# Agent attention with a gated convolution on one core: an earlier place for a four-column copy on GpSimd, another split of the last chunk, and eleven steps moved

## The chip, the cores and the metric

The kernel runs on one core of a Trainium2 chip. That core has five engines, each with its own instruction queue: TensorE (PE in the profile, its weight loads apart as PEld), VectorE (DVE), ScalarE (ACT), GpSimd (POOL) and SyncE (SP), which here issues nearly all DMA transfers. An engine works through its queue in order; semaphores order the engines against each other. The metric is the device time of one execution in microseconds; lower is better.

## The reference

There are 4 batches of 12800 tokens with 128 channels and 49 agent vectors. Agents attend over keys and values, queries attend over agents, and the result goes through a causal gated convolution of five taps and two projections:

```python
a2k = sm(agents, k); agent_v = a2k @ v      # 49 x 128 for a batch
x = sm(q, agents) @ agent_v                 # 12800 x 128 for a batch
gate_pre = sum(conv_w[k] * xp[:, k:k+S] for k in range(5))   # xp: x behind 4 rows of zeros
out = (1 / (1 + exp(-gate_pre)) * (x @ w_val)) @ w_out
```

`sm` is a softmax over scaled scores. All inputs are float32 (the weights of the second part arrive as float64).

## The kernel before

**Units.** A batch is cut into 10 units of 1280 tokens. Steps are named by a letter, the batch and the unit. `k1.4` takes scores of keys (16 matmuls, L376). `v1.4` exponentiates them and accumulates the agents' values (L480). `q1.4` takes scores of queries and makes their softmax: a 32x32 transposition on DVE (`sT`, L386), a maximum (`qmx`, L745), a subtraction on POOL (`qw`, L750), an exponential on ACT (L758), sums and a product on DVE (L763 to L772), and then three float16 pieces of the weights in a tile `pt`: a copy on ACT (L779) and two steps on POOL (L784, L794).

**Pairs.** `t1.4` turns `pt` so that agents lie on partitions and tokens along columns. The first four units use TensorE; all others use a DMA transposition issued by SP (L835), into half of a tile `x1`. One `x1` holds a pair of units, 2560 columns, behind 16 columns of padding; there are four such tiles. The convolution looks back over four tokens, so the last four columns of a pair must also stand ahead of the next pair's first column. A copy on POOL (L819; a memset, L816, at a batch's start) does this; it reads what the DMA transposition of the pair's second unit wrote, and so it waits for its landing. In the code this is `halo(s)`, for pair s. Behind the second unit of a pair, two shift DMAs (L884, `x2<-x1`) make five shifted copies of some rows for the whole pair; they too wait for the DMA transposition.

**Chunks.** The second part runs over 100 chunks of 512 tokens, 25 in a batch; five chunks make a pair. For chunk n, `g n` is six matmuls into the PSUM tile `gate` (five of L922, and L926, which reads `x2`) and a tanh on ACT (`th`, L935). `a n` is two matmuls into `val` (L949, L953), a product on DVE (`h`, L962), its float16 part on ACT (`hh`, L968) and the rest on POOL (`hl`, L973). `o n` is three matmuls (L992, L993 and L994, the last reading `hl`), a scaled copy on ACT (`ob`, L1006) and every other time a DMA to the output. The last chunk is cut into two of 256 columns, numbers 99 and 100. `gate`, `val` and `out` are single PSUM banks: `g n` waits for the tanh of the chunk before it, `a n` for its product.

**Folding.** Between two batches, `m` (maxima of the key scores, L425 to L457) and `f` (folding all weights into two stationary operands, L519 to L728) put short chains of DVE, POOL, ACT and PE steps on the way. `m2` first needs the maxima (`kmx`, L411) of all ten key units of batch 2.

**Order.** TensorE's order is written out by hand as one string of steps (`order`, in `tile_agent_attention_gated_conv`). Loads (L369, 640 KB each) follow from it: 11 buffers are filled in the order in which the `k`, `q` and `v` steps stand, and each load waits for the step that last used its buffer. For the other four engines and for SP, a planner (`Plan.order`) walks through the steps with given durations; when several are ready it takes the one with the longest remaining chain. A step becomes ready when all steps named as its reads have been placed, so a name in `reads` changes the order even where the data do not depend on it.

Of the kernel before, what the change touches and what calls it, by code (L numbers as in the profile page):

```python
# [13 lines left out]
ALU = mybir.AluOpType  # L14
# [8 lines left out]
UNIT = 1280  # L23
# [3 lines left out]
CH = 512  # L27
# [12 lines left out]
NT_, NH = 3, 3  # L40
NPT = 4
NX = 4
CUT = 2
NOB = 4
LEAD = 5
MAX_AT = (7, 8)
# [130 lines left out]
def tile_agent_attention_gated_conv(  # L177
# [9 lines left out]
    nc = tc.nc  # L187
    B, C, N = qT.shape
    A = 49
    NU = N // UNIT  # L190
    NCH = N // CH
    NT = B * NCH
# [606 lines left out]
    def on_pe(b, u):  # L799
        g = b * NU + u  # L800
        return g < PE_FIRST or (g < (B - 1) * NU and g % TURN in PE_TURNS)
# [11 lines left out]
    def halo(s):  # L813
        to = x1s[s % NX][:, PAD - HALO : PAD]
        if s * 2 % NU == 0:
            fn = lambda: nc.gpsimd.memset(to, 0.0)  # L816
            read = []
        else:
            fn = lambda: nc.gpsimd.tensor_copy(  # L819
                out=to, in_=x1s[(s - 1) % NX][:, PAD + SEG - HALO : PAD + SEG]  # L820
            )
            read = [(x, (s - 1) % NX, 1) for x in ("x1", "x1b")]

        read.append(("x2", (s - 1) % 3, UNIT, 0))
        add("pool", 0.1, fn, read, [("x1h", s % NX)])

    def transposes(b, u):
        g = b * NU + u
        pt = pts[g % NPT]
        p_ = ("pt", g % NPT)  # L830
        if not on_pe(b, u):
            dst = unit_rows(g)
            add(
                "dma", 1.4,
                lambda: nc.sync.dma_start_transpose(  # L835
                    out=dst.rearrange("p (n i) -> p n i", i=P),
                    in_=pt.rearrange("p n r -> p (n r)"),
                ),
                [(*p_, n) for n in range(3)], [("x1", g // 2 % NX, g % 2)], 2.4,
            )  # L840
            shifts(b, u)
            return
        ps_, at = bank()
        ps = ps_.rearrange("p a b -> p (a b)").bitcast(F16).rearrange("p (h w) -> p h w", h=2)
        dst = unit_rows(g).rearrange("p (h w) -> p h w", h=2)

        def matmuls():
            for n in range(NBLK):
                nc.tensor.transpose(
                    out=ps[:, n // HB, n % HB * P : (n % HB + 1) * P], in_=pt[:, n, :],  # L850
                    identity=ident16,
                )

        add("pe", 0.65, matmuls, [("pt", g % NPT, n) for n in range(3)], [at], key="t")
        add(
            "act", 0.65, lambda: nc.scalar.copy(out=dst[:, 0], in_=ps[:, 0, 0 : HB * P]),
            [at], [("x1", g // 2 % NX, g % 2)],
        )
        add(
            "dve", 0.46,  # L860
            lambda: nc.vector.tensor_copy(out=dst[:, 1], in_=ps[:, 1, 0 : HB * P]),
            [at], [("x1b", g // 2 % NX, g % 2)],
        )
        shifts(b, u)

    def shifts(b, u):

        g = b * NU + u
        if g >= SINGLE and g % 2 == 0:
            return  # L870
        n = 1 if g < SINGLE else 2
        u0 = u + 1 - n
        s = g // 2
        x2, x1 = x2s[s % 3], x1s[s % NX]
        o = (g + 1 - n) % 2 * UNIT
        src = row_keys(s, range(0, g % 2 + 1))
        c = PAD - HALO + o
        for r0, r1, every, us in X2CUTS:
            first = A + (2 if every == 3 else 3 * THREES)
            rows = x1[first : first + 1 + (r1 - r0 - 1) * every : every, c : c + 1]  # L880
            view = [rows.ap[0], (1, TAPS), (1, n * UNIT)]
            add(
                "dma", 0.6,
                lambda r0=r0, r1=r1, rows=rows, view=view: nc.sync.dma_start(  # L884
                    out=x2[r0 * TAPS : r1 * TAPS, o : o + n * UNIT],
                    in_=bass.AP(rows.tensor, rows.offset, view),
                ),
                src, [("x2", s % 3, o + i * UNIT, r0) for i in range(n)], us * n,
            )
        if g % 2 and (g + 1) // 2 < B * NU // 2:  # L890
            halo((g + 1) // 2)


    chunks = [(t // NCH, t % NCH * CH, CH) for t in range(NT - 1)]
    chunks += [(B - 1, N - CH + i * CH // CUT, CH // CUT) for i in range(CUT)]
    banks = {}

    def gates(t):
# [43 lines left out]
    def values(t):  # L942
# [5 lines left out]
        def matmuls():  # L948
# [19 lines left out]
            "act", 0.16 + 0.42 * scale, lambda: nc.scalar.copy(out=hh, in_=h),  # L968
            [("h", t % NH)], [("hh", t % 3)],
        )  # L970
        add(
            "pool", 0.1 + 1.07 * scale,
            lambda: nc.gpsimd.tensor_tensor(out=hl, in0=h, in1=hh, op=ALU.subtract),  # L973
            [("h", t % NH), ("hh", t % 3)], [("hl", t % 3)],
        )

# [101 lines left out]
    for t in range(len(chunks) + 2):  # L1078
# [8 lines left out]
    kinds = {"m": "max", "f": "fold"}  # L1087
    order = (
# [25 lines left out]
    )  # L1114
    first = [(kinds.get(x[0], x[0]), *map(int, x[1:].split("."))) for x in order.split()]
    for w in first:
# [70 lines left out]
```

## Time and profile before

| | us |
|---|---|
| median of 3 runs | 427.45 |
| lowest, highest | 425.69, 428.92 |
| the profiled execution | 425.66 |
| its span, first to last instruction | 423.6 |
| PE busy | 403.9 (95%) |
| ACT busy | 301.5 (71%) |
| DVE busy | 293.3 (69%) |
| POOL busy | 228.2 (54%) |

The profiled execution is 1.79 us below the median. The page gives busy times, the chain of work that ended last, and the waits by engine, line and releaser. The timeline gives single instructions: start, duration, engine, line, operation, tiles, and in brackets the idle time before it and what ended it. A row of SP (SPq) is the issue of a DMA, not its transfer. In the windows, a row is a stretch of time with the busy time of each engine, the clock granted to TensorE (PEclk, 1.00 is full), the busy share of the DMA engines and the rate they moved.

### The profile page before, as it was taken

The numbers are of one execution on the slowest core, as the hardware profiler recorded it, in microseconds if no ns is written. First come the engines' busy times: TensorE is split into PE (matmuls) and PEld (weight loads), VectorE is DVE, ScalarE is ACT, GpSimd is POOL, SyncE is SP. The second block draws the span as 40 slices with busy tenths as digits, with TensorE's granted clock in tenths as the row PEclk, the third lists the DMA queues.
The fourth block names the chain that finished last, engine by engine and source line by source line (L and its number), as shares of the span: only waits on it lengthen the run. The fifth ranks groups of instructions, "written<-read, shape, count | busy, mean of one in ns | idle before, by whom it ended". The sixth has DMA issues, their size and how long they took to land.

```text
span 423.6 us, 10042 instructions
## 1 busy us (share of the span) xinstructions
PE 403.9 (95%) x3907; PEld 197.0 (47%) x3907; DVE 293.3 (69%) x562; ACT 301.5 (71%) x521; POOL 228.2 (54%) x263
## 2 busy tenths in 40 slices
PE   4979999999999999999999899999999989999995
PEld 1358434346555443446555343335555534344443
DVE  3757899867875978667795575767765678676231
ACT  1564568779966777678876486778876567788776
POOL 1002557654657565554566355574366277877553
PEclk9969999999999999999999899999999999999998
DMA  8999999999999999999999999999999977755733
GB/s 320 420 417 411 370 367 353 301 295 310 412 293 283 346 317 362 304 278 356 351 379 324 271 299 370 314 332 302 296 393 322 239 196 161 199 163 176 205 121 124
DMA packets 75129, 127.62 MB, mean 301 GB/s; under 512 B 50466, under 2 KB 50850, under 8 KB 75084
## 3 DMA queue, kind: packets, MB, share of 16 engines
q1 hardware_dynamic: 74940, 126.87, 96.9%
q8 instruction: 30, 0.49, 0.5%
q10 hardware_dynamic: 144, 0.13, 0.2%
q14 instruction: 15, 0.12, 0.1%
HBM read 79.25 MB, written 26.21 MB: 249 GB/s over the span
## 4 chain that ended last, share of the span: by engine, by line
PE 78%; DMA 9%; DVE 8%; ACT 1%; POOL 1%; issue 1%; SPq 0%; POOLq 0%; DVEq 0%; ACTq 0%
PE gate L922 23%; PE sc L376 17%; PE av L480 10%; PE val L949 5%; PE out L992 5%; PE val L953 5%; PE gate L926 5%; PE out L993 4%; DMA ld<-kT 4%; PE out L994 4%; DMA x<-pt 3%; DMA x<-x 2%; DVE h L962 1%; DVE qw L772 1%; DVE qsm L763 1%
## 5 line engine op out<-in xcount | busy, mean ns | idle before, releaser
L973 POOL TENSOR_TENSOR hl<-h,hh 128x512 f16<-128x512 f32 (+1 forms) x101 | 116.9, 1158 | 96.1 <-ACT hh L968 96.0
L922 PE MATMUL gate<-x,stat 128*128 128x512 f16 (+1 forms) x500 | 125.2, 380 | 0.2 <-ACT th L935 0.2
L962 DVE SCALAR_TENSOR_TENSOR h<-th,val 128x512 f32<-128x512 f32 x100 | 67.8, 678 | 66.8 <-PE out L993 26.2
L376 PE MATMUL sc<-ld,ag_sb 128*32 128x320 f32 x1280 | 101.5, 447 | 7.6 <-DMA ld<-kT 7.0
L935 ACT ACTIVATE th<-gate,unscale 128x512 f32<-128x512 f32 x100 | 68.3, 683 | 33.3 <-PE gate L926 31.7
L1006 ACT ACTIVATE ob<-out,oscale 128x512 f32<-128x512 f32 x98 | 67.3, 687 | 21.3 <-PE out L994 20.1
L922 PEld LDWEIGHTS <-stat 128*128 128x128 f16 x505 | 46.3, 97 | 63.7 <-issue 14.8
L968 ACT CAST hh<-h 128x512 f16<-128x512 f32 (+1 forms) x101 | 61.5, 609 | 17.2 <-DVE h L962 16.4
L750 POOL TENSOR_TENSOR qw<-sT,qmx 128x490 f32<-128x490 f32 x40 | 41.4, 1035 | 47.6 <-DVE qmx L745 47.5
L376 PEld LDWEIGHTS sc<-ld,ag_sb 128*32 128x32 f32 x1280 | 36.7, 111 | 59.4 <-issue 25.7
L480 PE MATMUL av<-ld,eT 128*32 128x129 f32 (+1 forms) x1400 | 50.7, 279 | 1.0 <-DVE eT L386 1.0
L480 PEld LDWEIGHTS av<-ld,eT 128*32 128x32 f32 (+1 forms) x1400 | 47.1, 117 | 7.5 <-issue 2.5
L794 POOL TENSOR_TENSOR pt<-qw,pt 128x490 f16<-128x490 f32 x40 | 44.8, 1120 | 3.1 <-ACT pt L779 2.9
L471 ACT ACTIVATE e<-ks,kbias 128x320 f32<-128x320 f32 x80 | 39.3, 554 | 5.4 <-DVE eT L386 3.3
L386 DVE STREAM_TRANSPOSE sT<-sc 128x640 f32<-128x640 f32 x40 | 33.6, 839 | 13.4 <-PE sc L376 12.7
L402 ACT COPY ks<-sc 128x640 f32<-128x640 f32 x40 | 27.7, 691 | 21.2 <-PE sc L376 19.1
L386 DVE STREAM_TRANSPOSE eT<-e 128x640 f32<-128x640 f32 x40 | 33.5, 842 | 9.8 <-ACT e L471 5.2
L926 PE MATMUL gate<-x,stat 95*128 95x512 f16 x100 | 38.3, 383 | 1.5 <-DMA x<-x 1.5
L949 PE MATMUL val<-x,stat 128*128 128x512 f16 x100 | 38.2, 382 | 0.8 <-DVE h L962 0.6
L953 PE MATMUL val<-x,stat 95*128 95x512 f16 x100 | 38.1, 381 | 0.0
L994 PE MATMUL out<-hl,wo 128*128 128x512 f16 x98 | 37.0, 378 | 1.1 <-POOL hl L973 1.1
L992 PE MATMUL out<-hh,wo 128*128 128x512 f16 x98 | 37.3, 381 | 0.1
(130 smaller groups left out, 389.4 us busy)
## 6 DMA issues: line engine op xcount, KB each, us to landing
ld<-kT SPq DMA_DIRECT2D x40, 640.0 KB
ld<-qT SPq DMA_DIRECT2D x40, 640.0 KB
ld<-vP SPq DMA_DIRECT2D x39, 645.0 KB
outT<-ob SPq DMA_DIRECT2D x48, 512.0 KB
x<-x SPq DMA_DIRECT2D x18, 375.0 KB
x<-x SPq DMA_DIRECT2D x18, 100.0 KB
outT<-ob SPq DMA_DIRECT2D x3, 256.0 KB
x<-x SPq DMA_DIRECT2D x4, 187.5 KB
```

What stands on the lines that cost most here:

```text
L376: nc.tensor.matmul(out=out[g * BLK : (g + 1) * BLK, j, 0:GT], lhsT=ag_sb[:, b, j * BLK : (j + 1) * BLK], rhs=src[:, g * GT : (g + 1) * GT] ...
L386: nc.vector.transpose(out=out.rearrange("p n (j i) -> p j n i", j=2), in_=in_.rearrange("p j (n i) -> p j n i", i=BLK),)
L480: nc.tensor.matmul(out=av[o + j : o + j + cols, 0 : C + 1], lhsT=et[:, n, j : j + cols], rhs=vt[:, n, :], start=(u == 0 and n < 2), stop=( ...
L922: nc.tensor.matmul(out=pg, lhsT=stat[:, k, :], rhs=x1[:, c : c + w], start=(k == 0), stop=False,)
L926: nc.tensor.matmul(out=pg, lhsT=stat[0 : TAPS * X2R, TAPS + 1, :], rhs=x2[0 : TAPS * X2R, o2 : o2 + w], start=False, stop=True,)
L935: lambda: nc.scalar.activation(out=th, in_=pg, func=AF.Tanh, scale=unscale[:, 0:1]),
L949: nc.tensor.matmul(out=pv, lhsT=stat[:, TAPS, :], rhs=x1s[(b * NCH + n0 // CH) // 5 % NX][:, PAD + o2 : PAD + o2 + w], start=True, stop=False,
L953: nc.tensor.matmul(out=pv, lhsT=stat[0 : TAPS * X2R, TAPS + 2, :], rhs=x2[0 : TAPS * X2R, o2 : o2 + w], start=False, stop=True,)
L962: lambda: nc.vector.scalar_tensor_tensor(out=h, in0=th, scalar=1.0, in1=pv, op0=ALU.add, op1=ALU.mult),
L968: "act", 0.16 + 0.42 * scale, lambda: nc.scalar.copy(out=hh, in_=h),
L973: lambda: nc.gpsimd.tensor_tensor(out=hl, in0=h, in1=hh, op=ALU.subtract),
L1006: lambda: nc.scalar.activation(out=ob[:, o : o + w], in_=po, func=AF.Copy, scale=oscale),
```

## The change

**The copy of four columns.** `halo(s)` was added behind the shift DMAs of pair s-1, with a read that named these DMAs. It is now added at the start of `transposes` of the pair's first unit, and the name it reads is the `pt` of that unit as written by L794. So the planner places the copy behind POOL's work on the first unit of pair s. What it copies and what it truly waits for (the landing of the second unit of pair s-1) are the same.

**The end.** The two last chunks have 384 and 128 columns, and their `hl` is made by DVE.

**The order.** Eleven places in the string differ, and DMA issues and planner choices follow.

```diff
-CUT = 2
+CUTS = (384, 128)
@@ halo
-        read.append(("x2", (s - 1) % 3, UNIT, 0))
+        read.append(("pt", 2 * s % NPT, 1))
         add("pool", 0.1, fn, read, [("x1h", s % NX)])
@@ transposes
+        if g % 2 == 0 and g:
+            halo(g // 2)
@@ shifts
-        if g % 2 and (g + 1) // 2 < B * NU // 2:
-            halo((g + 1) // 2)
@@ chunks
-    chunks += [(B - 1, N - CH + i * CH // CUT, CH // CUT) for i in range(CUT)]
+    chunks += [(B - 1, N - sum(CUTS[i:]), w) for i, w in enumerate(CUTS)]
@@ values
+        on, eng, us = (nc.vector, "dve", 0.53) if t >= NT - 1 else (nc.gpsimd, "pool", 1.07)
         add(
-            "pool", 0.1 + 1.07 * scale,
-            lambda: nc.gpsimd.tensor_tensor(out=hl, in0=h, in1=hh, op=ALU.subtract),
+            eng, 0.1 + us * scale,
+            lambda: on.tensor_tensor(out=hl, in0=h, in1=hh, op=ALU.subtract),
@@ order (one of the eleven)
-"o35 t1.9 g38 a38 o36 g39 a39 o37 v2.4 t2.0 q2.1 v2.5 g40 a40 o38 q2.2 g41 a41 o39 "
+"o35 t1.9 g38 a38 o36 g39 a39 q2.1 o37 v2.4 t2.0 v2.5 g40 a40 o38 q2.2 g41 a41 o39 "
```

The other ten: `f0` behind `k1.1` instead of ahead of `q0.1`; `q0.6` ahead of `a3 o1`; `q1.4` ahead of `k2.2`; `o44` ahead of `f2 g46 a46`; `k3.2 k3.3` behind `o48`; `o50 k3.5` ahead of `t2.5`; `q2.8 k3.8` ahead of `g56`; `t3.0` ahead of `o62`; `a72` ahead of `o70`; `o96` ahead of `a98`.

Two places show what this makes of the queues. The first is POOL around the copy for pair 8 (units 1.6 and 1.7). The row `hl2` is that of chunk 29, the row `hl0` that of chunk 30; `x1_0` is the tile of pair 8, `x1_3` that of pair 7, `qw1` and `pt1` belong to unit 1.7, `pt0` to unit 1.6. Before:

```order
L794 TENSOR_TENSOR pt0_97<-qw0_89,pt0_97 128x10x49
L973 TENSOR_TENSOR hl1_118<-h1_112,hh1_115 128x512
L973 TENSOR_TENSOR hl2_119<-h2_113,hh2_116 128x512
L750 TENSOR_TENSOR qw1_90<-sT1_86,qmx1_88 128x490
L973 TENSOR_TENSOR hl0_117<-h0_111,hh0_114 128x512
L819 COPY x1_0_101<-x1_3_104 128x4
```

In the changed kernel:

```order
L794 TENSOR_TENSOR pt0_97<-qw0_89,pt0_97 128x10x49
L975 TENSOR_TENSOR hl1_118<-h1_112,hh1_115 128x512
L975 TENSOR_TENSOR hl2_119<-h2_113,hh2_116 128x512
L819 COPY x1_0_101<-x1_3_104 128x4
L750 TENSOR_TENSOR qw1_90<-sT1_86,qmx1_88 128x490
L975 TENSOR_TENSOR hl0_117<-h0_111,hh0_114 128x512
```

The copy moved ahead of the subtraction for query unit 1.7 and of `hl` of chunk 30.

The second place is SP's queue around the pair 9 (units 1.8 and 1.9, tile `x1_1`, shifted into `x20`); `x1_2` belongs to pair 10. Before:

```order
L835 DMA_TRANSPOSE x1_1_102<-pt2_99 128x10x128
L369 DMA ld10_71<-kT 128x1280
L835 DMA_TRANSPOSE x1_1_102<-pt3_100 128x10x128
L1021 DMA outT<-ob3_123 128x1024
L369 DMA ld0_61<-kT 128x1280
L369 DMA ld1_62<-qT 128x1280
L884 DMA x20_105<-x1_1_102 75x1x2560
L884 DMA x20_105<-x1_1_102 20x1x2560
L835 DMA_TRANSPOSE x1_2_103<-pt0_97 128x10x128
L835 DMA_TRANSPOSE x1_2_103<-pt1_98 128x10x128
```

In the changed kernel:

```order
L837 DMA_TRANSPOSE x1_1_102<-pt2_99 128x10x128
L369 DMA ld10_71<-qT 128x1280
L369 DMA ld0_61<-kT 128x1280
L837 DMA_TRANSPOSE x1_1_102<-pt3_100 128x10x128
L1023 DMA outT<-ob3_123 128x1024
L369 DMA ld1_62<-kT 128x1280
L837 DMA_TRANSPOSE x1_2_103<-pt0_97 128x10x128
L886 DMA x20_105<-x1_1_102 75x1x2560
L886 DMA x20_105<-x1_1_102 20x1x2560
L837 DMA_TRANSPOSE x1_2_103<-pt1_98 128x10x128
```

The load of query unit 2.5 moved ahead of the DMA transposition of unit 1.9, and the DMA transposition of unit 2.0 ahead of the two shift DMAs of pair 9.

20 rows, old and new, of the table order are left out of this document.

## The prediction

> **What bounds the kernel now.** I read the page first.
>
> ```profile
> span 423.6 us, 10042 instructions
> PE 403.9 (95%) x3907; PEld 197.0 (47%) x3907; DVE 293.3 (69%) x562; ACT 301.5 (71%) x521; POOL 228.2 (54%) x263
> DMA  8999999999999999999999999999999977755733
> ```
>
> TensorE is busy for 403.9 of 423.6 us; no other engine is above 71%. The change adds no matmul, so it can only act on PE's waits and on the clock PE is granted. The DMA engines are nearly full until four fifths of the span (32 of 40 slices, about 339 us): until then a transfer lands late, and an engine that waits for one waits long. So I asked next for the waits, by engine and releaser (total us, count, longest):
>
> ```profile
> PE sc L376 <- DMA ld<-kT: 7.0, 4, 6.1
> PE gate L926 <- DMA x<-x: 1.5, 1, 1.5
> PE out L994 <- POOL hl L973: 1.1, 1, 1.1
> PE val L949 <- DVE h L962: 0.6, 1, 0.6
> POOL x L819 <- DMA x<-pt: 16.4, 5, 6.0
> ```
>
> The first is mostly the first load (6.1), which stays. The next three are single stops of PE: A (1.5), B (1.1), C (0.6). The last is the copy that the change moves: it holds POOL for 16.4 us in five places, waiting for a DMA transposition.
>
> What a stop costs beyond its length shows in the windows (start, length, busy PE, PEld, DVE, ACT, POOL, clock, DMA share, GB/s):
>
> ```profile
> 233.57:236.98 3.41, 1.91 (x11) 1.02 (x10) 1.10 (x4) 1.43 (x3) 0.53 (x1) 1.00 1.26 190
> 236.98:240.40 3.42, 3.42 (x9) 1.18 (x9) 2.01 (x7) 1.30 (x2) 1.84 (x3) 0.50 1.05 335
> 339.38:342.80 3.42, 2.67 (x24) 1.29 (x24) 1.24 (x6) 1.63 (x4) 3.42 (x5) 1.00 0.56 149
> ```
>
> Stop A lies in the first row. In the next 3.42 us the clock is 0.50 and only 9 matmuls run: half of 3.42, 1.7 us, is lost. Behind B, in the third row, the clock stays at 1.00. So I charge 1.7 us of clock to a stop of 1.5 us or more, nothing to one of 1.1 or less, and A costs 1.5 + 1.7 = 3.2.
>
> The Trainium skill, "TensorE: Matmul & The Clock Gate", section "HAM oscillation — how this bites in real kernels", puts the limit at PE-idle gaps above about 3.4 us. By that rule A would cost 1.5 and the stop forecast below 2.1: the sum stays −1.3, since both lose 1.7, but the second rival below would be worth −3.4 instead of −5.1 and the third +0.5 instead of +2.2. The trace disagrees: a stop of 1.50 us is followed by a window at 0.50.
>
> **The change part by part.** *The copy for pair 8* (units 1.6 and 1.7). POOL, SP, ACT, DVE and PE around it:
>
> ```profile
> 173.60 1.16 POOL L973 TENSOR_TENSOR hl<-h,hh 128x512 f16<-128x512 f32 x1 [0.98 <-ACT hh L968]
> 176.85 1.02 POOL L750 TENSOR_TENSOR qw<-sT,qmx 128x490 f32<-128x490 f32 x1 [2.09 <-DVE qmx L745]
> 178.38 1.16 POOL L973 TENSOR_TENSOR hl<-h,hh 128x512 f16<-128x512 f32 x1 [0.51 <-ACT hh L968]
> 180.02 0.19 POOL L819 COPY x<-x 128x4 f16<-128x4 f16 x1 [0.47 <-issue]
> 179.97 1.68 SPq L884 DMA_DIRECT2D x<-x  x2
> 178.21 0.61 ACT L758 ACTIVATE qw<-qw 128x490 f32<-128x490 f32 x1
> 179.79 0.69 ACT L935 ACTIVATE th<-gate,unscale 128x512 f32<-128x512 f32 x1 [0.97 <-PE gate L926]
> 180.57 0.69 DVE L962 SCALAR_TENSOR_TENSOR h<-th,val 128x512 f32<-128x512 f32 x1 [0.36 <-PE out L993]
> 184.74 0.17 DVE L425 TENSOR_REDUCE m<-kmx 128x2 f32<-128x20 f32 x1
> 185.40 0.27 PE L432 MATMUL av<-ident,m 128*2 128x128 f32 x1
> ```
>
> Before, POOL does the subtraction of unit 1.7 (176.85) and `hl` of chunk 30 (178.38) ahead of the copy, and at 180.02 the copy no longer waits for its source. The shift DMAs wait for the same landing and are issued at 179.97, so I put it there. In the changed kernel the copy stands right behind `hl` of chunk 29, which ends at 173.60 + 1.16 = 174.76: POOL is held for 5.2 us. The subtraction then starts at 180.2 instead of 176.85 and ends at 181.2. ACT's exponential (178.21 before) starts at about 181.25 and ends at 181.86; the tanh of chunk 31 stands behind it and slips from 179.79 to 181.86, by 2.1 us. The product `h` behind it slips from 180.57 to about 183.0. DVE goes through the rest of its queue 2.1 to 2.6 us late up to the maximum at 184.74 (it also gets the exponential's sums later), and PE's L432, at 185.40 directly behind it, waits. Price 2.1 (up to 2.6, down to 0 if the landing comes 3.3 us earlier), and as it is above 1.5 another 1.7 for the clock: **+3.8**. What would cover it is work that PE has ready ahead of L432, and I see none beyond what runs anyway.
>
> *Stop A and SP's queue at pair 9.* SP and PE at the stop, and the same kinds of transfer later in a nearly idle queue:
>
> ```profile
> 220.73 2.63 SPq L835 DMA_TRANSPOSE x<-pt  x1
> 225.49 0.73 SPq L369 DMA_DIRECT2D ld<-qT  x1
> 228.28 1.65 SPq L884 DMA_DIRECT2D x<-x  x2
> 230.04 5.71 SPq L835 DMA_TRANSPOSE x<-pt  x2
> 235.67 0.39 PE L926 MATMUL gate<-x,stat 95*128 95x512 f16 x1 [1.50 <-DMA x<-x]
> 376.80 1.35 SPq L835 DMA_TRANSPOSE x<-pt  x1
> 381.08 1.65 SPq L884 DMA_DIRECT2D x<-x  x2
> ```
>
> The shift DMAs of pair 9 are issued at 228.28 and land at 235.67. Behind them stand two DMA transpositions (230.04); the change puts the first of these, unit 2.0, ahead of the shifts. Its price is not shown alone there: at least the issue of one in the nearly idle queue, 1.35, at most from its issue to the shifts that wait for it, 381.08 − 376.80 = 4.3. I take 2.2, nearer to the issue, since other engines' transfers overlap most of the 4.3. Against it, the copies stand elsewhere and transpositions of neighbouring units no longer go out in pairs, so the queue may run ahead: 0 to 2 us, I take 0.7. Loads keep their place: that of unit 2.5's queries passes one transposition but stood ahead of the shifts before too. So the shifts land at 235.67 + 2.2 − 0.7 ≈ 237.2, between 235.67 + 1.35 − 2 ≈ 235.0 and 235.67 + 4.3 = 240.0.
>
> PE wanted them at 235.67 − 1.50 = 234.17. By the parts above and below it now comes there 0.2 + 3.8 later, at 238.2, behind the landing: A goes, **−3.2**.
>
> The Trainium skill, "DMA: Bandwidth & Descriptors", section "Latency and other measured facts", gives 261 GB/s for a DMA transposition; a unit is 128 x 1280 float16, 0.33 MB, an estimate by that page of 1.26 us. No run here shows one by itself. It would leave the sum as it is, and shorten the wait of the first rival from 2.3 to 1.4.
>
> *Stops B and C.*
>
> ```profile
> 338.78 0.19 POOL L819 COPY x<-x 128x4 f16<-128x4 f16 x1 [5.99 <-DMA x<-pt]
> 338.93 2.27 POOL L973 TENSOR_TENSOR hl<-h,hh 128x512 f16<-128x512 f32 x2
> 341.15 0.61 POOL L541 TENSOR_TENSOR gw<-avT,moe_sb 128x245 f32<-128x245 f32 x1
> 345.56 0.64 DVE L962 SCALAR_TENSOR_TENSOR h<-th,val 128x512 f32<-128x512 f32 x1
> ```
>
> The copy of pair 16 holds POOL for 5.99 us until 338.78; `hl` of chunk 69 comes behind it and PE waits 1.1 (B). POOL's `gw` of the last fold is late too (341.15), DVE's fold chain behind it, and the product at 345.56 for which PE waits 0.6 (C). In the changed order that `hl` stands ahead of the copy, so both go: **−1.7**. If the fold chain still starts late, C stays (0.6).
>
> *The other copies.* Those for pairs 9 and 14 lose their holds, those for 6 and 7 gain 1 to 3 us, which the following `hl` has to spare; 12, 13 and 16 hardly move. I cost them at nothing, the cover being the time between `hl` and L994; if it is gone, a hold appears as a PE stop at L994, as at B.
>
> *Start.* `f0` behind `k1.1`:
>
> ```profile
> 42.38 0.42 PE L564 MATMUL val<-avT,moe_sb 128*128 128x49 f32 x2
> 45.03 0.79 PE L659 MATMUL gate<-ident,wst 128*128 128x128 f16 x8
> 56.44 0.99 PE L376 MATMUL sc<-ld,ag_sb 128*32 128x320 f32 x9 [0.58 <-DVE sT L386]
> ```
>
> The second fold step (between 42.38 and 45.03) comes one key unit later, so that the weights for the first chunk come about 0.8 late, and the 0.58 wait at 56.44 goes: **+0.2** (−0.6 to +0.8). The other moved names change the order of steps whose data are there; nothing.
>
> *End.*
>
> ```profile
> 418.23 0.42 DVE L962 SCALAR_TENSOR_TENSOR h<-th,sc 128x256 f32<-128x256 f32 x1 [1.00 <-ACT th L935]
> 419.30 0.67 POOL L973 TENSOR_TENSOR hl<-h,hh 128x256 f16<-128x256 f32 x1 [0.89 <-ACT hh L968]
> 420.33 0.47 ACT L1006 ACTIVATE ob<-sc,oscale 128x256 f32<-128x256 f32 x1 [0.62 <-PE sc L994]
> ```
>
> The last `hl` takes 0.67 on POOL for 256 columns; DVE needs 0.42 for the product of the same size, and 128 columns are half of it. The tail after the last product shrinks by about 0.67 − 0.25 = 0.4, while the piece of 384 ahead of it is longer by half: **−0.4** (−0.8 to +0.2).
>
> Sum: 0.2 + 3.8 − 3.2 − 1.7 − 0.4 = −1.3. On the profiled execution (425.66, 1.79 below the median) that gives 424.4; the same step from the median, 427.45 − 1.3 ≈ **426.2**.
>
> **The rivals.** *First: no stop at pair 8, but A stays.* If the transposition lands 3 us earlier than 179.97, the hold ends before the maximum is late (at most 0.5). For it: the release may have come earlier than SP's issue. Then PE is at the shifts at 234.17 + 0.2 + 0.5 = 234.9, the landing is 237.2, the wait 2.3 + 1.7 clock. Sum: 0.2 + 0.5 + (4.0 − 3.2) − 1.7 − 0.4 = −0.6, 426.9.
>
> *Second: neither stop.* If in addition the shifts run 2.3 us ahead, −3.2 falls out whole and nothing replaces it: 0.2 − 3.2 − 1.7 − 0.4 = −5.1, 422.4. Against it: the DMA engines are full up to 339 us, so a PE that is early meets its loads; I expect some 2 us of it to come back there, so 422.4 to 424.5.
>
> *Third, slower: both stops.* It decides when the transposition of unit 2.0 costs its upper bound and the shifts land at 240.0: PE, there at 238.2, waits 1.8 and the clock halves again, 1.7. From −1.3 that is +3.5: +2.2, 429.6. It needs a landing over 1.1 us behind PE for a stop of more than 1.1, so a price above about 3.
>
> *Fourth: the edits do not show.* The queue's transfers set when PE moves, and moves in the order are absorbed: 427.45.
>
> **How the numbers follow.** Forecast 0.35, first rival 0.25, second 0.20, third 0.15, fourth 0.05. The likeliest gives 426.2. One per cent, about what a measurement of this kernel can tell from no change, is 4.3 us: only the second rival at its full size, with an end or a start at its better bound, is faster by that (423.2 or less), 0.12; slower (431.7 or more) needs the third with the bounds of the start, the end and pair 8 on its side, or a stop that I don't see, 0.09; within, 0.79. The range runs from between the second rival's two ends, 422.8, to the third's 429.6 and 0.8 for the start: 430.4.
>
> **What would show it.** Pair 8: a POOL wait of about 5 us at L819 near 175, a PE wait of about 2 us at L432 near 185 and a clock row of 0.50 behind it; no such wait refutes the first term, and the size of POOL's hold tells the landing. Pair 9: no PE wait on the shift DMAs near 238 (a wait of 2 us there is the first rival, of nearly 2 us behind a stop at pair 8 the third). B and C: no PE wait at L994 or L949 between 338 and 347; if B is there, the hold of POOL was not its cause or has moved. End: from the last product to the last `ob` 0.4 shorter. A time under 423 would mean that the waits removed were worth their full length and that full DMA engines gave nothing back; one over 430.4, a stop that none of these rows shows.

## The result and the profile after

The changed kernel takes 431.48 us (median of 10 executions, 429.42 to 433.45), the kernel before 427.63 beside it (10 executions, 423.48 to 428.92). The ratio is 1.0106, 95% interval 1.0079 to 1.0134: slower by about 1%, where the forecast was 426.2 and its range ended at 430.4. The ratios here and below leave out executions over 1.5% above the fastest of the same kernel, the medians don't. The profiled execution took 431.97 us.

The page of the changed kernel, the same rows as of before:

```profile
span 429.9 us, 10039 instructions
PE 404.1 (94%) x3907; PEld 195.1 (45%) x3907; DVE 296.7 (69%) x564; ACT 300.5 (70%) x521; POOL 227.2 (53%) x261
DMA  8999999999999999999999999999999977655633
```

PE has the same work as before and waits longer. DVE is busy 3.4 us longer (the two `hl` of the end are its own now) and is still far from full. PE's waits, and POOL's for the copy (total us, count, longest):

```profile
PE sc L376 <- DMA ld<-kT: 8.3, 4, 6.3
PE gate L926 <- DMA x<-x: 5.0, 2, 4.2
PE gate L922 <- ACT th L935: 2.7, 2, 2.5
PE av L432 <- DVE m L425: 1.1, 1, 1.1
POOL x L819 <- DMA x<-pt: 20.0, 8, 5.3
```

Stops A, B and C of before (1.5, 1.1, 0.6) are gone. In their place stand a stop of 4.2 on shift DMAs, one of 2.5 on a tanh and one of 1.1 on the maximum; the copy holds POOL in eight places instead of five, for 20.0 us instead of 16.4.

**Pair 2.** The 4.2 is not at pair 9, where the forecast expected a stop, if any, but at pair 2. SP's queue and PE there before:

```profile
70.87 0.35 SPq L1021 DMA_DIRECT2D outT<-ob  x1
71.32 0.38 SPq L369 DMA_DIRECT2D ld<-qT  x1
73.26 5.94 SPq L835 DMA_TRANSPOSE x<-pt  x1
79.94 2.68 SPq L835 DMA_TRANSPOSE x<-pt  x1
86.20 1.68 SPq L884 DMA_DIRECT2D x<-x  x2
93.97 0.38 PE L926 MATMUL gate<-x,stat 95*128 95x512 f16 x1
```

In the changed kernel, with PE's stop:

```profile
71.87 5.71 SPq L837 DMA_TRANSPOSE x<-pt  x1
77.68 4.12 SPq L1023 DMA_DIRECT2D outT<-ob  x1
81.91 0.37 SPq L369 DMA_DIRECT2D ld<-qT  x1
82.37 2.12 SPq L837 DMA_TRANSPOSE x<-pt  x1
88.60 1.67 SPq L886 DMA_DIRECT2D x<-x  x2
97.09 0.39 PE L926 MATMUL gate<-x,stat 95*128 95x512 f16 x1 [4.25 <-DMA x<-x]
```

The transposition of unit 0.4 now goes out ahead of a store and of a load; the store behind it takes 4.12 us to issue, that of unit 0.5 follows at 82.37 (79.94 before) and the shifts at 88.60 (86.20 before). Their last packets land at 96.2 in the trace (93.1 before), and the semaphore that PE waits for is complete at 97.0 (93.7 before). PE is 1.1 us earlier there than before and finds nothing. The windows around the stop and its clock:

```profile
94.07:97.49 3.42, 0.40 (x5) 0.18 (x9) 0.00 (x0) 0.00 (x0) 0.03 (x1) 1.00 1.26 227
97.49:100.90 3.41, 3.41 (x44) 2.08 (x48) 1.06 (x2) 3.01 (x6) 1.16 (x1) 0.50 0.95 290
```

**Pair 8.** POOL, ACT, DVE and PE:

```profile
184.78 0.19 POOL L819 COPY x<-x 128x4 f16<-128x4 f16 x1 [4.89 <-DMA x<-pt]
184.93 1.01 POOL L750 TENSOR_TENSOR qw<-sT,qmx 128x490 f32<-128x490 f32 x1
185.97 0.61 ACT L758 ACTIVATE qw<-qw 128x490 f32<-128x490 f32 x1 [2.54 <-POOL qw L750]
186.50 0.67 ACT L935 ACTIVATE th<-gate,unscale 128x512 f32<-128x512 f32 x1
191.54 0.17 DVE L425 TENSOR_REDUCE m<-kmx 128x2 f32<-128x20 f32 x1
191.77 0.27 PE L432 MATMUL av<-ident,m 128*2 128x128 f32 x1 [1.08 <-DVE m L425]
```

This is the chain that was forecast, step by step: copy held 4.89 (forecast 5.2), subtraction late, exponential late, tanh behind it, maximum, PE.

**Pair 9.** The transposition of unit 2.0, then the shifts, then PE:

```profile
229.42 3.66 SPq L837 DMA_TRANSPOSE x<-pt  x1
233.38 1.65 SPq L886 DMA_DIRECT2D x<-x  x2
240.59 0.38 PE L926 MATMUL gate<-x,stat 95*128 95x512 f16 x1
```

The shifts are issued 5.1 us later than before (228.28). Their last packets land at 239.3 and the semaphore is complete at 240.3 (235.6 before). PE comes at 240.59 and doesn't wait, because by now it is itself 6.6 us late.

**Pair 16.** SP's issue of the transposition of unit 2.8, POOL at the copy, ACT and PE:

```profile
314.92 6.10 SPq L837 DMA_TRANSPOSE x<-pt  x1
344.95 0.19 POOL L819 COPY x<-x 128x4 f16<-128x4 f16 x1 [5.34 <-DMA x<-pt]
346.21 0.60 POOL L541 TENSOR_TENSOR gw<-avT,moe_sb 128x245 f32<-128x245 f32 x1
347.35 0.40 ACT L644 COPY wst<-wst 128x245 f16<-128x245 f16 x1 [3.71 <-DVE wst L607]
348.46 0.68 ACT L935 ACTIVATE th<-gate,unscale 128x512 f32<-128x512 f32 x1
349.19 1.47 PE L922 MATMUL gate<-x,stat 128*128 128x512 f16 x5 [2.50 <-ACT th L935]
```

The transposition of 2.8 before:

```profile
301.94 1.84 SPq L835 DMA_TRANSPOSE x<-pt  x1
```

In the changed kernel the seven transfers from 307.81 on stand ahead of it that stood behind it before, and three more stand ahead of that of unit 2.7 (issued at 296.20, 290.88 before). All later ones are late, that of unit 3.1 lands at 344.1 (338.3 before; PE itself is 3.2 late by then), and the copy holds POOL until 344.95. `hl` of chunk 69 is now ahead of the copy, but the last fold's `gw` is still behind it; ACT waits 3.71 for what DVE makes of it, with the tanh of chunk 72 queued behind.

How far the changed profile lies behind that of before, at PE's L926: −1.1 at chunk 1, +4.8 at chunk 11 (pair 2), +5.1 at 25, +6.3 at 34 (pair 8), +6.6 at 43, +3.1 at 47 (A gone), +3.2 at 69, +6.1 at 75 (pair 16), and +6.3 at the end of the span.

### The profile page after: what moved, and what is told of

Same layout as the page of the kernel before. It is cut to its first block, busy times and chain, and to the rows that moved or that the text cites. A ratio compares the mean times of both kernels' runs of the same rounds, so it can differ in the third digit from the quotient of the medians.

```text
span 429.9 us, 10039 instructions
## 1 busy us (share of the span) xinstructions
PE 404.1 (94%) x3907; PEld 195.1 (45%) x3907; DVE 296.7 (69%) x564; ACT 300.5 (70%) x521; POOL 227.2 (53%) x261
## 4 chain that ended last, share of the span: by engine, by line
PE 70%; DMA 13%; DVE 8%; ACT 4%; issue 2%; POOL 1%; SPq 0%; ACTq 0%; DVEq 0%; POOLq 0%
PE gate L922 20%; PE sc L376 14%; PE av L480 9%; DMA x<-pt 5%; DMA ld<-kT 5%; PE val L949 4%; PE out L994 4%; PE val L953 4%; PE gate L926 4%; PE out L995 4%; PE out L996 4%; DMA x<-x 3%; DVE h L962 1%; ACT th L935 1%; DVE kmx L411 1%
## 5 line engine op out<-in xcount | busy, mean ns | idle before, releaser
L975 POOL TENSOR_TENSOR hl<-h,hh 128x512 f16<-128x512 f32 x99 | 116.2, 1174 | 90.3 <-ACT hh L968 88.4
L376 PE MATMUL sc<-ld,ag_sb 128*32 128x320 f32 x1280 | 103.2, 453 | 8.6 <-DMA ld<-kT 8.3
L480 PE MATMUL av<-ld,eT 128*32 128x129 f32 (+1 forms) x1400 | 49.3, 277 | 0.6 <-DVE eT L386 0.6
L480 PEld LDWEIGHTS av<-ld,eT 128*32 128x32 f32 (+1 forms) x1400 | 45.7, 115 | 7.9 <-issue 2.8
L794 POOL TENSOR_TENSOR pt<-qw,pt 128x490 f16<-128x490 f32 x40 | 44.4, 1109 | 7.5 <-ACT pt L779 7.3
L926 PE MATMUL gate<-x,stat 95*128 95x512 f16 x100 | 38.3, 383 | 5.0 <-DMA x<-x 5.0
L949 PE MATMUL val<-x,stat 128*128 128x512 f16 x100 | 38.2, 382 | 0.2 <-DVE h L962 0.2
L994 PE MATMUL out<-hh,wo 128*128 128x512 f16 x98 | 37.5, 383 | 0.1
L996 PE MATMUL out<-hl,wo 128*128 128x512 f16 x98 | 37.0, 378 | 0.3 <-POOL hl L975 0.3
```

Source lines behind the costliest of these rows:

```text
L376: nc.tensor.matmul(out=out[g * BLK : (g + 1) * BLK, j, 0:GT], lhsT=ag_sb[:, b, j * BLK : (j + 1) * BLK], rhs=src[:, g * GT : (g + 1) * GT] ...
L480: nc.tensor.matmul(out=av[o + j : o + j + cols, 0 : C + 1], lhsT=et[:, n, j : j + cols], rhs=vt[:, n, :], start=(u == 0 and n < 2), stop=( ...
L926: nc.tensor.matmul(out=pg, lhsT=stat[0 : TAPS * X2R, TAPS + 1, :], rhs=x2[0 : TAPS * X2R, o2 : o2 + w], start=False, stop=True,)
L949: nc.tensor.matmul(out=pv, lhsT=stat[:, TAPS, :], rhs=x1s[(b * NCH + n0 // CH) // 5 % NX][:, PAD + o2 : PAD + o2 + w], start=True, stop=False,
L975: lambda: on.tensor_tensor(out=hl, in0=h, in1=hh, op=ALU.subtract),
```

## The experiments

In the edits, a name in quotes is a step of the order string, and a line of dots stands for code left out. Theory Q stands for SP's queue, K for the copy, D for the full DMA engines.

| run | kernel | median us | ratio, 95% interval |
|---|---|---|---|
| e1 | changed, q0.6 back | 428.54 | 1.0040 (1.0007 to 1.0073) |
| e2 | changed, q2.8 k3.8 back | 428.25 | 1.0030 (1.0009 to 1.0052) |
| e3 | changed, copy in its old place | 430.35 | 1.0060 (1.0033 to 1.0087) |
| e4 | before, copy alone moved | 427.38 | 1.0007 (0.9969 to 1.0046) |
| e5 | changed, q0.6 and q2.8 k3.8 back | 426.46 | 0.9994 (0.9967 to 1.0021) |
| e6 | before, q0.6 alone moved | 427.25 | 1.0023 (0.9998 to 1.0048) |
| e7 | before, f0 alone moved | 426.59 | 0.9996 (0.9968 to 1.0024) |
| e8 | before, the end alone | 426.13 | 0.9988 (0.9965 to 1.0011) |
| e9 | before, late copy | 422.99 | 0.9911 (0.9879 to 0.9943) |
| e10 | e9, shifts of pair 9 first | 427.67 | 0.9960 (0.9921 to 0.9999) |
| e11 | e10, f0 and end | 425.44 | 0.9977 (0.9956 to 0.9998) |
| e12 | changed, a second profile | 429.24 | one execution |
| e13 | changed, late copy | 428.54 | 1.0049 (1.0032 to 1.0066) |
| e14 | e13, q0.6 and q2.8 k3.8 back | 426.13 | 0.9979 (0.9949 to 1.0009) |
| e15 | e9, f0 and end | 424.15 | 0.9940 (0.9916 to 0.9965) |
| e16 | e14, q2.1 and k3.2 k3.3 back too | 423.86 | 0.9941 (0.9912 to 0.9970) |
| e17 | e9, q2.1 and k3.2 k3.3 moved | 426.62 | 0.9976 (0.9946 to 1.0007) |
| e18 | e17, a second profile | 428.08 | one execution |

### The two moved places

e1 and e2 each undo one place of the order in the changed kernel; e5 both.

```diff
-"a2 t0.3 t0.4 g3 q0.6 a3 o1 g4"
+"a2 t0.3 t0.4 g3 a3 o1 q0.6 g4"
```

```diff
-"a55 q2.8 k3.8 g56 o54 a56 g57"
+"a55 g56 o54 a56 q2.8 k3.8 g57"
```

> The changed kernel with query unit 0.6 back behind a3 o1 in the order. Theory Q (SP's queue): its early place put the DMA transposition of unit 0.4, the first of all, ahead of a store and of a load, the one of 0.5 behind them, and so the shift DMAs of pair 2 landed 3.1 us later. Then PE's wait of 4.25 at 92.84 falls to 1.2 or less, the clock stays at 1.00 behind it, and the time is 431.5 - 4.2 - 1.7 = 425.6; up to 428 if the stop on pair 9's shifts comes back, since PE is 6 us earlier there. Theory K (the copy's new place makes every new stop by holding POOL): 431.5, the stop stays.

> The changed kernel with q2.8 k3.8 back behind a56. Theory Q: their early place put the DMA transposition of unit 2.8 behind seven transfers, so that the one of 3.1 landed at 344.1 (338.3 before). Undone, it lands some 4 us earlier against PE, the wait of 2.50 for the tanh at 346.69 goes with its clock drop: 431.5 - 2.5 - 1.7 = 427.3. The copy of pair 16 then stands ahead of hl of chunk 69 again, so a wait of up to 1.1 at the last matmul of chunk 69 may return: up to 428.5. The stop of 4.25 near 93 stays. Theory K: the copy holds POOL as long as before, 431.5.

> The changed kernel with both q0.6 and q2.8 k3.8 back in their old places. Theory Q (each of the two moves makes a stop of its own, independent of the other): the gains of the two single runs add, 431.5 - 2.9 - 3.2 = 425.4; no wait above 1.2 near 93 and none of the tanh near 346; a wait of 1 to 2 for the maximum near 188 stays. Theory D (the full DMA engines set the pace up to about 337 us, so that what one stop loses another one gives back): the gains don't add, 427.5 to 428.5, and a wait on shift DMAs or loads stands where none was before.

In e1 the transposition of 0.4 is back behind the store and the load; PE's wait at pair 2 is 0.88 and the clock stays at 1.00 there. In e2 the wait for the tanh near 347 is gone, and waits of 0.54 (L996) and 0.58 (L949) stand there instead, about as before. PE at pair 2 in e1, and at pair 8 in e5:

```profile
95.31 0.38 PE L926 MATMUL gate<-x,stat 95*128 95x512 f16 x1 [0.88 <-DMA x<-x]
187.61 0.27 PE L432 MATMUL av<-ident,m 128*2 128x128 f32 x1 [1.91 <-DVE m L425]
```

Each place is worth about 3 us at the median. Together they give 5.0 of the 6.2 that would be their sum, and bring the changed kernel to the time of before. That speaks for theory Q, and no new wait on shift DMAs, which theory D asked for, stands in e5's profile. What it doesn't give is the forecast gain: e5 waits 1.9 for the maximum of pair 8, as forecast.

e6 moves q0.6 alone in the kernel before.

> The kernel before with only q0.6 moved. Theory Q: the shift DMAs of pair 2 land at about 96 to 97 and PE, there at about 94, waits 2.3 to 3.3, with 1.7 of clock in some executions; but PE then comes later to the shifts of pair 9, so that stop A shrinks or goes (-1.5, -1.7). 427.5 to 430. Theory C (the place of the copy for pair 3, or the earlier f0, is needed for the stop): no stop above 1 near 94, 427.

There was no stop at pair 2 (0.50), but one of 2.42 at the shifts of pair 4, which neither theory had expected. The load of q1.0 stays ahead of the transposition here; only with f0 moved too do both, store and load, fall behind it. That the long stop at pair 2 needs both moves is likely, but rests on this one profile.

### The copy

e3 puts the copy of the changed kernel back, as shown; e4 moves it alone in the kernel before, the reverse edit.

```diff
-        read.append(("pt", 2 * s % NPT, 1))
+        read.append(("x2", (s - 1) % 3, UNIT, 0))
...
-        if g % 2 == 0 and g:
-            halo(g // 2)
...
+        if g % 2 and (g + 1) // 2 < B * NU // 2:
+            halo((g + 1) // 2)
```

> The changed kernel with the copy of four columns in its old place (behind the shift DMAs); the order and the end are the changed ones. Theory Q: the stop of 4.25 near 93 stays. The DMA transposition of 3.1 still lands at about 344, and the copy now stands ahead of hl of chunk 69, so PE waits about 344.9 + 1.2 + 1.2 - 342 = 4 to 5 there instead of 2.5: slower by some 2. The wait of 1.07 for the maximum near 191 goes: -1.2. Sum 431 to 433. Theory K: both new stops go with the copy, 425 to 426.

> The kernel before with only the copy's new place. Theory Q: no stop near 93 on the shifts, none of 2.5 near 346; stops A (1.5, with its clock drop) and B (1.1) stay. At pair 8 the copy stands even ahead of hl of chunk 29, so that this and the subtraction are late: a PE wait of 1 to 3 between 180 and 187, with 1.7 of clock if it is 1.5 or more in one piece. 428.5 to 432. Theory K: the stops of 4.25 and 2.5 appear here too, over 433.

In e3 the wait for the maximum is gone, and PE waits 5.30 at pair 9's shifts. The stop near 93 was 1.43 instead of 4, with the same SP order, and the wait at L996 of chunk 69 was 0.83 instead of 4 to 5; theory Q had expected none of the three. Theory K's 425 to 426 didn't come either: e3 takes 430.35. In e4 (PE's waits; total us, count, longest):

```profile
PE out L996 <- POOL hl L975: 3.5, 2, 2.7
```

2.68 of it are at chunk 29, whose `hl` stood behind the held copy, with the clock at 0.50 afterwards; stop A is gone. One stop stands for the other and the time is that of before.

e12 is a second profile of the changed kernel, because of the 1.43.

> The changed kernel once more, for a second profile. If SP's hold at the store o1 behind the first DMA transposition belongs to this order of the queue, the wait at pair 2's shifts is 3 to 4.5 again. If it falls differently from one execution to the next (1.4 in the run with the copy in its old place, the same SP order), it can be 1 to 2. The wait for the tanh near 347 is 2 to 3 in either case. 430 to 433.

Its waits of PE, and POOL's copy for pair 8:

```profile
PE av L432 <- DVE m L425: 2.0, 1, 2.0
PE gate L922 <- ACT th L935: 1.8, 3, 1.2
PE gate L926 <- DMA x<-x: 1.3, 2, 1.1
183.13 0.19 POOL L819 COPY x<-x 128x4 f16<-128x4 f16 x1 [6.31 <-DMA x<-pt]
```

The store behind the first transposition took 0.5 to issue and the wait at pair 2 was 1.1. The same order gave 4.25, 3.61 (e2), 1.43 (e3), 1.07 (e12) and 0.83 (e13), and only in the first two did the store take over 4 us to issue. So the 4.25 belongs to some executions; what holds SP there in one and not in the other isn't settled. The wait for the tanh was 1.2, and the time below the 430 expected. At pair 8 the wait was 2.02 with a clock drop, the whole term 4.3 us (from +2.1 at chunk 30 to +6.4 at 34). From chunk 34 to 69 the two executions agree within 0.1 us, and both are 3.2 behind before at chunk 69; at chunk 75 this one is at +3.4, the first at +6.1.

### The copy later still

e9 makes one edit to the kernel before: the copy stands behind POOL's work on the pair's second unit, when its source has long landed. e13 and e14 do it in the changed kernel and in e5. The edit is shown against the changed kernel's place of the copy.

```diff
-        if g % 2 == 0 and g:
+        if g % 2 and g > 3 or g == 2:
             halo(g // 2)
...
-        read.append(("pt", 2 * s % NPT, 1))
+        read.append(("pt", (2 * s + (s > 1)) % NPT, 1))
```

> The kernel before, the copy of four columns placed behind POOL's work on the second unit of the pair instead of its first (pair 1 behind its first, and the memsets with them); nothing else. If the copy's waits on POOL are what makes B and C: no POOL wait at the copy anywhere, no PE wait at L996 near 340 (1.1) nor at L949 near 346 (0.6), A (1.5 to 2.4, with its clock drop in part of the executions) stays: 427 - 1.7 = 425.3. Rival (the full DMA engines give it back, or fold steps come late by themselves): 426.5 to 427.5, and a wait remains near 340 to 350.

> The changed kernel with the copy one unit later still (behind POOL's work on the pair's second unit), order and end unchanged. If the holds of POOL by the copy carry the pair-8 wait (1.1 to 2.0, with a clock drop in part of the executions) and the tanh wait near 347 (1.2 to 2.5), both go: 431.5 - 2 - 3 = 426 to 427, and the wait at pair 2's shifts (1.1 to 4.3) stays; stop A can come back, since PE is then earlier at pair 9. If the moved steps of the order make the loss by themselves (late transpositions, whoever waits for them), it stays at 429 to 431.

> The changed kernel with q0.6 and q2.8 k3.8 back and the late copy: 426.5 without the late copy. The wait for the maximum near 186 (1.9, with a clock drop) goes, that at L949 near 346 (0.6) too: 426.5 - 3.6 = 423; with PE 3.6 earlier at pair 9 (it had 3.0 to spare) a wait of up to 1 there comes back: 423 to 424.5. If the other moved steps and the end were worth something, it is below the 423.0 of the kernel before with the late copy; if not, equal.

In e9 POOL waits 0.3 for the copy instead of 16.4, and B and C are gone; A stays (waits of POOL, then of PE):

```profile
POOL x L819 <- DMA x<-pt: 0.3, 1, 0.3
```

```profile
PE gate L926 <- DMA x<-x: 4.2, 3, 2.3
```

With 422.99 it beats both kernels. It gains more than the 1.7 expected for B and C, 3.4 at the medians. Between chunks 69 and 75 its profile gains 2.0; where the rest comes from it doesn't show. e13 has no hold, no wait for the maximum, no wait for the tanh, and one large stop:

```profile
240.25 0.61 PE L926 MATMUL gate<-x,stat 95*128 95x512 f16 x1 [5.41 <-DMA x<-x]
```

This is pair 9, and the order makes it: without the copy's holds PE is on time, and the last packets of the shifts land at 239.7. e14 has 4.44 there and isn't told from e5.

### Which moves make pair 9 late

e16 undoes two more places in e14, as shown; e17 makes only these two in e9, the reverse edit. e18 is a second profile of e17.

```diff
-"g39 a39 q2.1 o37 v2.4 t2.0 v2.5 g40"
+"g39 a39 o37 v2.4 t2.0 q2.1 v2.5 g40"
...
-"o47 t2.4 g50 q2.5 f2 a50 o48 k3.2 k3.3 g51"
+"o47 t2.4 k3.2 k3.3 g50 q2.5 f2 a50 o48 g51"
```

> The run with the late copy and both places undone, and two more undone: q2.1 and k3.2 k3.3 (with o48). On SP the load of q2.5 is back behind the DMA transposition of 1.9 and the one of 2.0 behind the shifts of pair 9. If these two moves are what makes pair 9's shifts land at 239 to 240: landing 235 to 236.5, the wait at A 0.5 to 2.4 instead of 4.4, time 422.5 to 424. If the landing is late for another reason (the end, f0, the rest of the order): 425.5 to 427, the wait stays above 3.

> The kernel before with the late copy (423.0) and only those two moves of the order. If they make pair 9's shifts late by themselves: landing 238.5 to 240, a wait at A of 4 to 5.4 with a clock drop, time 425.5 to 427. If not: landing 236.6 as without them, 423.

> The same kernel as the run before (late copy, the two moves q2.1 and k3.2 k3.3), for a second profile: its times lay between 422.4 and 429.3 and the profiled execution was the fastest of them, with a wait of only 0.9 at pair 9's shifts. If the two moves act through that wait, an execution near the median of 426.6 shows a wait of 3 or more there, with the shifts landing at 238 or later; if its time is near 427 with a wait below 2 there, they act elsewhere.

e16: last packets of the shifts at 234.5, wait 0.93, median 423.86; its interval overlaps that of e14. e17: median 426.62, against 422.99 without the two moves (e9), and the intervals are apart, so the moves cost what was expected; but the profiled execution was its fastest (422.43), with the last packets at 234.6 and a wait of 0.92. The second profile, at 428.08, shows the stop, and both windows behind it at half clock:

```profile
239.89 0.61 PE L926 MATMUL gate<-x,stat 95*128 95x512 f16 x1 [5.23 <-DMA x<-x]
```

The two executions have the same queue; the DMA stream of the second lies 3 to 5 us behind from pair 8 on.

All profiles together separate the moves from the DMA stream. From the last packet of unit 1.8's transposition to the completed semaphore of pair 9's shifts it takes 12.7 to 14.2 us in all ten profiles with q2.1 and k3.2 k3.3 moved, and 10.2 to 12.0 in the eight with them in their old places (e10 and e11 apart). So the moves make the landing about 2 us later. The rest is the DMA stream: unit 1.8's last packet lies between 222.3 and 227.6, with and without the moves.

### The rest

e7 moves f0, e8 makes the end alone (with "o96" ahead of "a98" and `hl` of the last two on DVE), e15 both in e9.

```diff
-"f0 t0.0 f0 q0.1 k1.0 f0 k1.1 f0 q0.2"
+"f0 t0.0 q0.1 k1.0 f0 k1.1 f0 f0 q0.2"
...
-CUT = 2
+CUTS = (384, 128)
```

> The kernel before with only the fold step f0 moved behind k1.1. By the prediction +0.2. By the profile of the changed kernel PE is 1.1 earlier at chunk 1 in spite of a first wait on loads that was 1.3 longer there; then chunk 1 comes 1 to 2 earlier, but stop A grows by the part that the shift DMAs of pair 9 don't move with it: 425.5 to 427.2.

> The kernel before with only the end changed (384 and 128 columns, hl of both on VectorE, o96 ahead of a98). By the prediction -0.4 (-0.8 to +0.2). By the profile of the changed kernel the last matmul comes 0.8 earlier against chunk 98, but from it to the end of the last store's packets it takes 2.7 instead of 1.9: +0.0 to +0.3, 426.9 to 427.3.

> The kernel before with the late copy, f0 behind k1.1 and the changed end, all loads and shifts in their old places. The three parts add: 423.0 - 0.2 - 0.7 = 422.1 (421 to 423), stop A stays (1.5 to 2.4). If f0 only moves PE against a queue that doesn't follow, A or the wait at pair 2 grows by as much: 423 to 424.

None of the three is told from zero: e15 against e9 is 1.2 slower at the medians, with intervals that overlap. e7's profile shows why an earlier PE isn't worth anything there: 1.2 us earlier at chunk 1, it waits 1.05 at pair 2 and is where it was before; at A it waits 1.56.

e10 issues pair 9's shifts (`early_shifts`) ahead of the two loads in front of them, k3.3 and q2.5 (`late_loads`), with the late copy; e11 adds f0 and the end.

```diff
-    for i in plan.order():
+    todo = plan.order()
+    for i in late_loads:
+        todo.remove(i)
+    at = 1 + max(todo.index(i) for i in early_shifts)
+    todo[at:at] = late_loads
+    for i in todo:
         plan.steps[i][2]()
```

> As the run with the late copy, and the two shift DMAs of pair 9 issued ahead of the two loads (k3.3, q2.5) that stand in front of them on SP. Theory Q: the shifts land some 2 to 3 us earlier than 234.5, A goes with its clock drop: 425.3 - 1.5 - (0 to 1.7) = 422.1 to 423.8. Theory D (the full DMA engines set the pace): the two loads are 3 us later and what A gave comes back as a wait on loads or on the next shifts: 425 or more.

> As the run before, with the fold step f0 behind k1.1 and the changed end (384 and 128, hl of both on VectorE, o96 ahead of a98). Each alone measured -0.2 and -0.7 (neither clear of zero). Theory Q: 421.5 to 423.5; theory D: 424.5 to 425.5.

A goes, and both are slower than e9 at the median. By the ratios only e11 is told from e9; e10's interval overlaps that of e9, and its executions reach from 421.88 to 429.68. This leans to theory D, but in e10's profile the loss is neither a wait on loads nor one on the next shifts: the copy for pair 13 is held again, 3.06 us, and the chain of pair 8 appears a second time, at the last fold's maximum:

```profile
288.21 0.19 POOL L822 COPY x<-x 128x4 f16<-128x4 f16 x1 [3.06 <-DMA x<-pt]
288.36 1.01 POOL L753 TENSOR_TENSOR qw<-sT,qmx 128x490 f32<-128x490 f32 x1
291.71 0.27 PE L435 MATMUL av<-ident,m 128*2 128x128 f32 x1 [3.38 <-DVE m L428]
```

## Why the prediction was wrong

**The step that failed** is the sentence at the end of the start's term, "The other moved names change the order of steps whose data are there; nothing." For two of the moved names that was false, on a queue that the prediction had followed in one place only. q0.6 (with f0) puts the first DMA transposition ahead of a store and a load, q2.8 k3.8 that of unit 2.8 behind seven transfers. Each costs about 3 us at the median (e1, e2). Undoing both gives 426.46, against a forecast of 426.2. That the numbers are so near is partly luck: e5's ratio of 0.9994 (0.9967 to 1.0021) shows no gain, and its profile has +3.7 at pair 8, −3.5 at A and −0.8 at B and C, where −1.7 was forecast. PE's slack at pair 2's shifts was 0.3 us in the profile of before (semaphore complete at 93.7, PE there at 94.0), so comparing every shift DMA's landing with PE's L926, not only the one that already made it wait, would have shown the place.

How the moves act is shown less firmly than that they do. In the second profile of the changed kernel the same two places show less, +1.3 at pair 2 and +0.2 at pair 16, and another 1.7 us are lost at chunks 22 to 24, which no run here explains.

**Stops B and C, −1.7**: wrong. `hl` of chunk 69 was indeed moved ahead of the copy, but `gw` was not, and the copy's source landed 5.9 us later, with PE 3.2 late itself. The stop went from L994 to the tanh: +2.9 in the first profile, +0.2 in the second (+3.2 to +6.1 and to +3.4 between chunks 69 and 75). The wait for the tanh stands in the three profiles that have both q2.8 k3.8 early and the copy in its new place (2.50, 1.88 in e1, 1.20 in e12) and in no other. The prediction named `gw` as the cause of C and left it behind the copy. With the late copy both stops go, −2.0 in e9.

**Pair 8, +3.8**: right in its mechanism; the size is right where the clock drops. Measured +1.2 (wait 1.08, no drop) and +4.3 (2.02 and a drop); e1, e2 and e5 have +1.8 (1.67, no drop), +2.1 (2.01, no drop) and +3.7 (1.91 and a drop).

**Stop A, −3.2**: right in size, −3.5 in both profiles, but in part by luck. The forecast counts the landing as the moment at which PE is let go (235.67 before). That is when the semaphore is complete, at 240.3 and 238.7, not 237.2; the first is beyond the upper bound of 240.0. The stop is gone all the same because PE, forecast there at 238.2, comes at 240.6, made late by stops that the sum didn't have. In e5, without these, the term holds as it was meant: semaphore at 235.6, PE there at 238.1. "Loads keep their place" is what was mis-sized: the load of q2.5 stood ahead of the shifts before, but now stands ahead of the transposition of 1.9, which the shifts wait for. The last packet of 1.9 lands 5.7 us behind that of 1.8 in the changed profile and 4.1 in that of before (232.8 and 227.7). The third rival's late landing is real (240.2 in e13, with a stop of 5.41); in the changed kernel it is hidden since PE is late by other stops. Take these away and it appears: e3, e13, e14.

**Start, +0.2**: not confirmed. Against the profile of before, chunk 1 comes 1.1 and 0.9 earlier, though PE's waits on loads are 1.3 and 1.5 longer in all; but the seven profiles of other runs with f0 in its old place come 0.4 to 0.7 earlier too. On the time it has no effect that is told from zero (e7).

**End, −0.4**: +0.2 in the profile, where the last three results queue on ACT; alone −0.7 at the median, not told from zero.

**The clock, 1.7 for a stop of 1.5 or more**: too simple, below. The sum of the changes, −1.3, was thus a sum over the places followed; most of the loss lies outside them.

## What to carry to other kernels

When an order is changed, follow every DMA on its queue, and list for each wait that PE could have how much later the transfer may land before PE sees it: here pair 2, which had 0.3 us to spare and showed no stop, cost 5.9 us in one profile and 1.3 in the other, and the visible stop A was worth 3.5. A step that waits for a transfer and shares an in-order engine with the critical path should be placed where its source has long landed: one unit later made the copy's 16.4 us of holds 0.3 and was worth 0.9% in the kernel before. Taking a stop from PE can come back at the next transfer that is late, as in e13, where PE on time met a stop of 5.41 at pair 9; in e9 it did not.

## What the runs showed of the hardware

**The clock goes by windows, not by the length of a stop.** The clock records of each trace lie on a grid of 3.41 us. In e2 a stop of 3.61 us at pair 2 spread over two windows, with PE busy 1.62 and 1.59 in them, and the clock stayed at 1.00. In e5 a stop of 1.91 us fell into one window, with PE busy 1.50, and the next window ran at 0.50:

```profile
91.42:94.83 3.41, 1.62 (x8) 0.53 (x6) 1.86 (x3) 2.23 (x5) 1.75 (x2) 1.00 1.07 313
94.83:98.24 3.41, 1.59 (x25) 0.81 (x29) 0.00 (x0) 1.10 (x3) 0.00 (x0) 1.00 1.14 180
98.24:101.65 3.41, 3.41 (x89) 2.55 (x79) 2.80 (x4) 2.91 (x7) 2.19 (x2) 1.00 1.43 334
```

```profile
184.61:188.02 3.41, 1.50 (x9) 0.57 (x7) 2.69 (x6) 3.06 (x6) 3.13 (x4) 1.00 1.04 212
188.02:191.44 3.42, 3.42 (x10) 1.19 (x9) 2.23 (x7) 1.82 (x3) 1.62 (x2) 0.50 1.14 287
```

Over all twenty profiles, between 30 and 415 us, the clock was halved behind 16 of the 17 windows with PE busy 1.53 us or less (not behind one of 1.48 in e10). Behind windows with 1.59 or more it was not, with two exceptions: 1.91 in the profile of before, and 2.76 in e1, in a window that itself ran at 0.50. The Trainium skill, "TensorE: Matmul & The Clock Gate", section "What's actually happening", says that the window is free-running; that agrees with the grid, whose place against the first instruction differs from trace to trace (1.5 us past a multiple of 3.41 before, 1.9 in the changed profile). The rule of its section "HAM oscillation — how this bites in real kernels", PE-idle gaps above about 3.4 us, does not agree: 1.91 was enough here, and 3.61 wasn't. So the same stop costs 1.7 us more in some executions than in others, and twice that where two windows are halved (e18).

**One order, several DMA streams.** The executions of e17 reach from 422.4 to 429.3; in its two profiles (e17, e18) the last packets of pair 8's shifts land at 205.5 and 209.7 and those of pair 9's at 234.6 and 239.3. Which transfer gives way isn't settled.

**DMA transpositions of one size take different times.** In the changed profile it was between 1.27 us (unit 2.0) and 7.5 us (the first, unit 0.4) from the first packet of one to its last; 20 of the 36 took 2.5 to 4.3, and those in the nearly idle queue at the end (3.4 to 3.9) 1.6 to 1.7. What makes the difference isn't shown. The shortest six (1.27 to 1.41) lie near the estimate of 1.26, which the prediction works out from the 261 GB/s that the Trainium skill, "DMA: Bandwidth & Descriptors", section "Latency and other measured facts", states for a transposition with a non-contiguous middle dimension; the other thirty are longer.
